# Start addresses of the x tiles in a fused gated attention and two-layer MLP kernel: four different residues of 512 bytes, or one

## The chip, the cores and the metric

One core of one Trainium2 chip runs the whole program. The metric is the device time of one execution in microseconds. Three runs of the kernel before gave 943.04, 944.69 and 944.89 us, median 944.69 us.

## The reference, cut to what matters

```python
f = 1.0 / (1.0 + np.exp(-f_logit))                      # q, k, v, f: (4, 8, 768, 48)
for t in range(S):
    state = f[:, :, t, :, None] * state + np.einsum('bhd,bhe->bhde', k[:, :, t], v[:, :, t])
    y[:, :, t] = np.einsum('bhd,bhde->bhe', q[:, :, t], state)
x = y.transpose(0, 2, 1, 3).reshape(3072, 384)
h = np.maximum(x @ w_in, 0.0)                           # (384, 2048)
x = h * h @ w_out                                       # (2048, 384)
h = x @ w2_in
g = np.where(h > 0.0, h, np.exp(np.minimum(h, 0.0)) - 1.0)
return g @ w2_out
```

The weights arrive as float64 and are decoded on the chip.

## The kernel before, in words

The 3072 tokens are cut into six blocks of 512, and each block passes through two layers. `BLOCKS` numbers them 0 to 5 (layer 0, whose x comes out of the attention) and 6 to 11 (layer 1, whose x is what layer 0 left in DRAM). Each block has 16 units, one for each 128 columns of the hidden width.

Precision is kept by splitting: x is held as a high and a low part (`xh`, `xl`, both of the type fp32r), so are the weights (`w`, `wf`) and the hidden values (`gh`, `gl`). A unit is 18 matmuls of TensorE, each with a stationary operand of 128 x 128 and a moving operand of 128 x 512:

- `up` (L343), nine matmuls into one PSUM bank `ph`: six whose moving operand is one of the three 512-column pieces of `xh`, each piece twice (with the high and the low weights), then three with the pieces of `xl`.
- `down` (L395), nine matmuls into three banks `y`: for each bank two with `gh` and one with `gl`.

Between the two, ScalarE, VectorE and GpSimd make `gh` and `gl` of `ph` (L356 to L382). The order of work is written out by hand. In slot u the loop at the end of `chunked` first runs what the table `plan` has for that slot (loads, the weights of layer 0 and 1, and a step of the chunked attention), then `up(u)`, then `down(u-2)`, then `between(u)` and `low(u)`. TensorE therefore sees up, down, up, down, and in layer 0 at some slots a piece of attention in front of `up`: either the scores (tp L166, sc L172) or the state and output (kv L201, y3p and yp L229 and L234).

The places in SBUF are set by the pools. A pool lays its tiles out one behind the other, and the pools follow each other in the order in which they are opened: `one`, `two`, `three`, `wpool`. The pool `two` gives every tag two buffers, so blocks with an even number use one `xh` and one `xl` buffer and odd blocks the other pair. `new_x` (L253 to L256) makes them: each tile has 16 columns of four bytes (64 bytes) more than it needs, and the views that the matmuls read begin behind these.

```python
tiles = [two.tile([128, NK * n + 16], F32R, tag=f"x{p}", name=f"x{p}{i}") for p in "hl"]
xr[i] = tuple(t[:, 16:].rearrange("r (k t) -> r k t", t=n) for t in tiles)
```

The views are filled by L263 and L269/L271 (layer 0) and by L280 and L281 (layer 1). The pieces within a view are 2048 bytes apart, so all three have the same residue.

Of the kernel before, what the change touches and what calls it, by code (L numbers as in the profile page):

```python
# [11 lines left out]
F32 = mybir.dt.float32  # L12
F32R = mybir.dt.float32r
# [12 lines left out]
NK = DM // 128  # L26
# [28 lines left out]
def chunked(ctx, tc, ff, qk, vk, vz, wraw, mask, ident, flag, out):  # L55
# [8 lines left out]

    one = ctx.enter_context(tc.tile_pool(name="one", bufs=1))
    two = ctx.enter_context(tc.tile_pool(name="two", bufs=2))
    three = ctx.enter_context(tc.tile_pool(name="three", bufs=3))
    wpool = ctx.enter_context(tc.tile_pool(name="wpool", bufs=NF))
    dram = ctx.enter_context(tc.tile_pool(name="dram", bufs=1, space=bass.MemoryType.DRAM))
# [11 lines left out]
    state = [one.tile([ROWS, NP, 48], F32, name=f"state{b}") for b in range(B)]  # L81
    diag = one.tile([ROWS, NP, ROWS], F32, name="diag")
    dlast = [one.tile([ROWS, NP], F32, name=f"dlast{b}") for b in range(B)]
    x2d = dram.tile([NK, 128, NT], F32, name="x2d")
    wst = dram.tile([NF, 128, 2, 2, DM], F32, name="wst")

    st = {}
    xr = {}
# [163 lines left out]

    def new_x(i):  # L253
        n = BLOCKS[i][2]
        tiles = [two.tile([128, NK * n + 16], F32R, tag=f"x{p}", name=f"x{p}{i}") for p in "hl"]
        xr[i] = tuple(t[:, 16:].rearrange("r (k t) -> r k t", t=n) for t in tiles)  # L256

    def a_hi(g):
        i, o = where[g]
        if o == 0:  # L260
            new_x(i)
        hi = xr[i][0][:, :, o:o + 128]
        A.activation(hi, st[g]["yp" if g < B else "x1"], AF.Copy)  # L263
# [9 lines left out]
    def load_x(i, k):  # L273
        layer, t0, n = BLOCKS[i]
        if k == 0:
            new_x(i)
        x = two.tile([128, n], F32, tag="x1", name=f"x2_{i}_{k}")
        nc.sync.dma_start(out=x, in_=x2d[k, :, t0:t0 + n])
        hi, lo = (a[:, k] for a in xr[i])
        V.tensor_copy(hi, x)  # L280
        V.tensor_tensor(out=lo, in0=x, in1=hi, op=ALU.subtract)  # L281
# [138 lines left out]
    for g in range(B, NG):  # L420
        i, o = where[g]
# [149 lines left out]
@with_exitstack  # L571
def gated_attention_moe(ctx: ExitStack, tc: tile.TileContext, ff, qk, vk, vz, nat, wraw, mask, ident, out):
    pool = ctx.enter_context(tc.tile_pool(name="flag", bufs=1))
    flag = pool.tile([1, 1], I32, name="flag")
    with ExitStack() as inner:
        chunked(inner, tc, ff, qk, vk, vz, wraw, mask, ident, flag, out)
    rv = tc.nc.values_load(flag[0:1, 0:1], min_val=0, max_val=1)
    with tc.If(rv == 1):
        with ExitStack() as inner:
            general(inner, tc, nat, wraw, ident, out)  # L580
# [56 lines left out]
```

## Time and profile before

| what | value |
|---|---|
| median of three runs | 944.69 us (943.04 to 944.89) |
| the profiled execution, device time | 943.66 us |
| its span, first to last instruction | 941.9 us |
| mean granted TensorE clock | 0.981 |
| PE busy, PEld busy | 913.2 us (97%), 740.8 us (79%) |
| VectorE, ScalarE, GpSimd busy | 564.4 us (60%), 455.8 us (48%), 327.1 us (35%) |
| chain that ended last, by engine | PE 87%, DVE 8%, issue 2% |

A matmul's duration in the profile overlaps that of the next one, so busy time says little about how close TensorE is to its rate. What is read below is the distance from the start of one matmul to the start of the next, which is the time that each one really takes of the program.

### The profile page before, as it was taken

The numbers are of one execution on the slowest core, as the hardware profiler recorded it, in microseconds if no ns is written. First come the engines' busy times: TensorE is split into PE (matmuls) and PEld (weight loads), VectorE is DVE, ScalarE is ACT, GpSimd is POOL, SyncE is SP. The second block draws the span as 40 slices with busy tenths as digits, with TensorE's granted clock in tenths as the row PEclk, the third lists the DMA queues.
The fourth block names the chain that finished last, engine by engine and source line by source line (L and its number), as shares of the span: only waits on it lengthen the run. The fifth ranks groups of instructions, "written<-read, shape, count | busy, mean of one in ns | idle before, by whom it ended". The sixth has DMA issues, their size and how long they took to land.

```text
span 941.9 us, 13099 instructions
## 1 busy us (share of the span) xinstructions
PE 913.2 (97%) x4841; PEld 740.8 (79%) x4841; DVE 564.4 (60%) x834; ACT 455.8 (48%) x791; POOL 327.1 (35%) x295
## 2 busy tenths in 40 slices
PE   6888989999999999999999999999999999999996
PEld 4766768888888888788888888888888888888885
DVE  8888886667667766775401166456555555555543
ACT  4457664554445445454444444444444444443543
POOL 5222323443444443444233232332332333233231
PEclk8799899999999999999999999999999999999998
DMA  8445423444433443442246530100100100100001
GB/s 277 141 141 192 131 67 123 135 137 141 141 108 109 143 142 126 154 146 78 94 158 213 174 135 1 57 12 1 56 12 1 56 13 0 57 12 1 34 0 37
DMA packets 30791, 88.44 MB, mean 94 GB/s; under 512 B 4992, under 2 KB 9728, under 8 KB 30720
## 3 DMA queue, kind: packets, MB, share of 16 engines
q1 hardware_dynamic: 28848, 77.32, 24.7%
q10 hardware_dynamic: 1872, 10.22, 3.2%
q8 instruction: 39, 0.64, 0.3%
q14 instruction: 32, 0.26, 0.1%
HBM read 64.52 MB, written 22.02 MB: 92 GB/s over the span
## 4 chain that ended last, share of the span: by engine, by line
PE 87%; DVE 8%; issue 2%; ACT 1%; DMA 1%; POOL 0%; ACTq 0%; DVEq 0%
PE y L395 40%; PE ph L343 40%; PE sc L172 2%; DVE dec L51 1%; DVE w L313 1%; PE yp L229 1%; PE yp L234 1%; DVE ds L136 1%; DVE dec L52 1%; PE kv L201 1%; DVE dec L48 1%; PE y3p L234 1%; DVE ss L181 1%; PE tp L166 1%; PE y3p L229 1%
## 5 line engine op out<-in xcount | busy, mean ns | idle before, releaser
L382 POOL TENSOR_TENSOR gl<-gg,gh 128x512 fp32r<-128x512 f32 x175 | 232.5, 1328 | 489.6 <-PE ph L343 193.5
L395 PE MATMUL y<-gh,w 128*128 128x512 f32 x576 | 179.9, 393 | 0.0
L395 PE MATMUL y<-gh,wf 128*128 128x512 f32 (+1 forms) x582 | 179.6, 390 | 0.0
L343 PE MATMUL ph<-xh,w 128*128 128x512 f32 x576 | 158.6, 410 | 11.2 <-ACT w L312 7.5
L368 DVE SCALAR_TENSOR_TENSOR t<-r,t 128x512 f32<-128x512 f32 (+1 forms) x97 | 71.5, 737 | 162.4 <-ACT r L367 161.3
L343 PE MATMUL ph<-xh,wf 128*128 128x512 f32 (+1 forms) x582 | 147.8, 389 | 0.0
L364 ACT ACTIVATE r<-ph 128x512 f32<-128x512 f32 (+1 forms) x97 | 57.6, 594 | 186.0 <-PE ph L343 176.7
L343 PEld LDWEIGHTS ph<-xh,w 128*128 128x128 f32 x576 | 107.1, 192 | 38.5 <-ACT w L312 9.2
L395 PEld LDWEIGHTS y<-gh,w 128*128 128x128 f32 x576 | 108.9, 189 | 24.9
L395 PEld LDWEIGHTS y<-gh,wf 128*128 128x128 f32 x582 | 108.9, 188 | 24.4 <-ACT gh L371 0.2
L343 PEld LDWEIGHTS ph<-xh,wf 128*128 128x128 f32 x582 | 108.6, 188 | 23.7
L395 PE MATMUL y<-gl,wf 128*128 128x512 f32 (+1 forms) x291 | 112.8, 388 | 0.0
L395 PE MATMUL y<-gl,w 128*128 128x512 f32 x288 | 112.5, 391 | 0.0
L356 ACT ACTIVATE r<-ph 128x512 f32<-128x512 f32 x96 | 56.9, 593 | 91.1 <-PE ph L343 73.5
L343 PE MATMUL ph<-xl,w 128*128 128x512 f32 x288 | 84.7, 403 | 0.2 <-DVE xl L269 0.2
L343 PE MATMUL ph<-xl,wf 128*128 128x512 f32 (+1 forms) x291 | 82.2, 391 | 0.0
L362 DVE TENSOR_TENSOR gh<-r 128x512 fp32r<-128x512 f32 x64 | 44.5, 696 | 48.6 <-ACT r L356 48.1
L369 DVE SCALAR_TENSOR_TENSOR gg<-ph,t 128x512 f32<-128x512 f32 (+1 forms) x97 | 66.6, 686 | 10.0
L343 PEld LDWEIGHTS ph<-xl,w 128*128 128x128 f32 x288 | 56.1, 195 | 13.2 <-DVE xl L269 0.6
L357 ACT ACTIVATE gg<-r 128x512 f32<-128x512 f32 x96 | 60.8, 633 | 8.0 <-ACT r L356 0.4
L395 PEld LDWEIGHTS y<-gl,wf 128*128 128x128 f32 x291 | 54.7, 188 | 12.1 <-DVE gl L376 0.2
L395 PEld LDWEIGHTS y<-gl,w 128*128 128x128 f32 x288 | 54.2, 188 | 12.4
(84 smaller groups left out, 1067.3 us busy)
## 6 DMA issues: line engine op xcount, KB each, us to landing
raw<-wraw SPq DMA_DIRECT2D x19, 768.0 KB, 4.5
wst<-w SPq DMA_DIRECT2D x16, 768.0 KB, 4.0
wf<-wst SPq DMA_DIRECT2D x16, 768.0 KB, 4.3
qk<-qk SPq DMA_DIRECT2D x24, 448.0 KB, 5.4
raw<-wraw ACTq DMA_DIRECT2D x13, 768.0 KB, 4.4
ff<-ff SPq DMA_DIRECT2D x22, 227.9 KB, 4.5
x2d<-yo SPq DMA_DIRECT2D x18, 256.0 KB, 2.3
x<-x2d SPq DMA_DIRECT2D x18, 256.0 KB, 3.1
```

The lines of the kernel that those rows point to most:

```text
L172: PE.matmul(sc[j][:, p], k[lo:hi, p], q[lo:hi, p], start=True, stop=True)
L229: PE.matmul(o[64 * j:64 * j + c.stop - c.start], v[:, c], ss[g % 2][:, j, p], start=p in (0, NK), stop=False, skip_group_check=True,)
L234: PE.matmul(o[:ROWS], diag[:, p], q[:, p], start=False, stop=p >= NK - 1, skip_group_check=True)
L343: PE.matmul(ph, w[:, a, 0, 128 * k:128 * k + 128], b[:, k, c], start=(m == 0), stop=(m == len(todo) - 1))
L356: A.activation(r[:, c], ph, AF.Relu)
L357: A.activation(gg[:, c], r[:, c], AF.Square)
L362: V.tensor_tensor(out=gh[:, c], in0=r[:, c], in1=r[:, c], op=ALU.mult)
L364: A.activation(r[:, c], ph, AF.Relu, scale=-1.0)
L368: V.scalar_tensor_tensor(out=t[:, c], in0=r[:, c], scalar=1.0, in1=t[:, c], op0=ALU.add, op1=ALU.mult)
L369: V.scalar_tensor_tensor(out=gg[:, c], in0=ph, scalar=0.0, in1=t[:, c], op0=ALU.max, op1=ALU.add)
L382: G.tensor_tensor(out=gl, in0=gg, in1=gh, op=ALU.subtract)
L395: PE.matmul(yp_[i][m][:, c], w[:, a, 1, 128 * m:128 * m + 128], b[:, c], start=(f == 0 and n_ == 0), stop=(f == NF - 1 and n_ == 2 and c.s ...
```

## The change

Two small tiles that nothing reads or writes are allocated, one of 64 bytes at the end of the part of the pool `one` that is laid out first, one of 192 bytes in a new pool `gap`, opened behind `two`. The x tiles lose their 64 bytes of margin.

```diff
     two = ctx.enter_context(tc.tile_pool(name="two", bufs=2))
+    gap = ctx.enter_context(tc.tile_pool(name="gap", bufs=1))
     three = ctx.enter_context(tc.tile_pool(name="three", bufs=3))
...
+    one.tile([128, 16], F32, name="shift")
+    gap.tile([128, 48], F32, name="shift2")
...
     def new_x(i):
         n = BLOCKS[i][2]
-        tiles = [two.tile([128, NK * n + 16], F32R, tag=f"x{p}", name=f"x{p}{i}") for p in "hl"]
-        xr[i] = tuple(t[:, 16:].rearrange("r (k t) -> r k t", t=n) for t in tiles)
+        tiles = [two.tile([128, NK * n], F32R, tag=f"x{p}", name=f"x{p}{i}") for p in "hl"]
+        xr[i] = tuple(t.rearrange("r (k t) -> r k t", t=n) for t in tiles)
```

No instruction is added, removed or moved: on every engine the sequence of operations, their shapes and the semaphores that they wait for are those of the kernel before. What differs is where operands start. The built programs place them so (start of the data, modulo 512 bytes):

| operand | before | after |
|---|---|---|
| `xh` of even blocks | 384 | 320 |
| `xl` of even blocks | 0 | 320 |
| `xh` of odd blocks | 320 | 320 |
| `xl` of odd blocks | 448 | 320 |
| `gh`, `gl` (all three buffers each), `yo` | 64 | 64 |
| weights `w`, `wf` (all sixteen buffers) | 64 | 64 |
| `qk` (both), the groups from 4 on | 256 | 320 |
| `vk`, `raw`, `dec`, `gg` (both buffers of each) | 0 | 320 |
| `ff` and `t` (first, second buffer) | 128, 192 | 192, 256 |
| `kt` | 352 | 416 |
| `r` | 96 | 160 |
| `x1` and `x2` staging (both) | 64 | 384 |
| `ss`, `diag`, `state`, `idt`, `msk`, `lim`, `ds` | unchanged | unchanged |

## Rows read from the trace of the kernel before

**Rows 1.** Busy time by stretch: us; PE, PEld, DVE, ACT, POOL busy (instructions); PEclk granted clock; DMA share, GB/s.
```profile
0.00:60.00 60.00, 46.77 (x354) 35.06 (x355) 50.41 (x73) 29.30 (x49) 22.24 (x30) 0.83 0.59 190
60.00:120.00 60.00, 54.82 (x341) 43.12 (x340) 52.70 (x81) 38.51 (x70) 20.72 (x19) 0.91 0.48 156
...
200.00:280.00 80.00, 80.00 (x490) 65.40 (x488) 54.06 (x80) 40.69 (x77) 34.30 (x35) 1.00 0.42 137
...
600.00:680.00 80.00, 80.00 (x351) 65.53 (x350) 44.99 (x69) 36.54 (x60) 24.66 (x19) 1.00 0.11 37
```

**Rows 2.** Chain of waits around 125 us: start us, us, engine, tile and line.
```profile
123.72 0.85 ACT w L312
124.60 0.97 DVE w L313
125.61 2.13 PE ph L343 x8
127.74 2.10 PE y L395 x9
```

**Rows 3.** TensorE in order of time, odd block 7: start us, us until the last end, group.
```profile
599.26 1.52 PE L343 MATMUL ph<-xh,wf 128*128 128x512 f32 x6
600.62 0.86 PE L343 MATMUL ph<-xl,wf 128*128 128x512 f32 x3
601.31 0.63 PE L395 MATMUL y<-gh,wf 128*128 128x512 f32 x2
...
602.01 0.62 PE L395 MATMUL y<-gh,wf 128*128 128x512 f32 x2
...
602.70 0.61 PE L395 MATMUL y<-gh,wf 128*128 128x512 f32 x2
...
603.38 0.39 PE L343 MATMUL ph<-xh,wf 128*128 128x512 f32 x1
```

**Rows 4.** The same view, first unit of even block 8.
```profile
665.18 1.55 PE L343 MATMUL ph<-xh,wf 128*128 128x512 f32 x6
666.57 0.85 PE L343 MATMUL ph<-xl,wf 128*128 128x512 f32 x3
667.26 0.63 PE L395 MATMUL y<-gh,wf 128*128 128x512 f32 x2
...
667.96 0.61 PE L395 MATMUL y<-gh,wf 128*128 128x512 f32 x2
...
668.64 0.61 PE L395 MATMUL y<-gh,wf 128*128 128x512 f32 x2
...
669.32 0.63 PE L343 MATMUL ph<-xh,wf 128*128 128x512 f32 x2
```

**Rows 5.** The same view, starts of blocks 6, 9, 10 and 11.
```profile
533.02 0.63 PE L343 MATMUL ph<-xh,wf 128*128 128x512 f32 x2
...
731.42 0.61 PE L343 MATMUL ph<-xh,wf 128*128 128x512 f32 x2
...
797.34 0.63 PE L343 MATMUL ph<-xh,wf 128*128 128x512 f32 x2
...
863.58 0.62 PE L343 MATMUL ph<-xh,wf 128*128 128x512 f32 x2
```

**Rows 6.** The same view, two groups of nine y matmuls behind each other, block 11.
```profile
927.52 0.62 PE L395 MATMUL y<-gh,wf 128*128 128x512 f32 x2
...
929.56 0.62 PE L395 MATMUL y<-gh,wf 128*128 128x512 f32 x2
...
931.60 0.40 PE L395 MATMUL y<-gh,wf 128*128 128x256 f32 x2
```

**Rows 7.** The same view, odd block 1, the unit behind an attention output.
```profile
180.92 0.85 PE L343 MATMUL ph<-xl,w 128*128 128x512 f32 x3
...
183.70 1.53 PE L343 MATMUL ph<-xh,w 128*128 128x512 f32 x6
185.06 0.86 PE L343 MATMUL ph<-xl,w 128*128 128x512 f32 x3
```

**Rows 8.** Chain of waits, attention pieces of one group of tokens each.
```profile
171.35 0.39 PE tp L166 x4
171.74 1.09 PE sc L172 x16
...
177.15 0.54 PE kv L201 x13
177.69 0.29 PE y3p L229 x4
177.98 0.66 PE yp L229 x12
178.64 0.40 PE y3p L234 x2
179.04 0.66 PE yp L234 x6
```

**Rows 9.** VectorE in order of time, t in two neighbouring units, so in both its buffers.
```profile
702.54 0.69 DVE L368 SCALAR_TENSOR_TENSOR t<-r,t 128x512 f32<-128x512 f32 x1 [2.12 <-ACT r L367]
...
706.68 0.69 DVE L368 SCALAR_TENSOR_TENSOR t<-r,t 128x512 f32<-128x512 f32 x1
```

**Rows 10.** Page, DMA issues: tiles, queue, count, KB each, us from issue to landing.
```profile
raw<-wraw SPq DMA_DIRECT2D x19, 768.0 KB, 4.5
...
wf<-wst SPq DMA_DIRECT2D x16, 768.0 KB, 4.3
```

## The prediction, made before the changed kernel was run

> **What bounds the kernel now.** I read the busy time by stretch first. From 200 us on PE is busy in all 80 of 80 us of a stretch at a granted clock of 1.00, the 2.4 GHz level, while DVE has 45 to 54 of 80 [rows 1]. In the first 120 us it is otherwise: PE is busy for 46.8 and 54.8 of 60 us, DVE for 50.4 and 52.7. The chain of waits agrees: it runs through the weight split on DVE up to 125.6 us and stays on PE from there [rows 2]. So a saving on PE counts from about 125 us to the end, and before that it counts nothing.
>
> A busy PE is not a PE at its best rate, so I went on to TensorE in order of time and took distances between starts. In odd block 7 the six matmuls on `xh` take 600.62 - 599.26 = 1.36 us, 226.7 ns each; the three on `xl` take 0.69; the nine on `gh` and `gl` take 603.38 - 601.31 = 2.07, in threes 0.70, 0.69 and 0.68 [rows 3]. The unit takes 4.12 us. In even block 8 the six take 1.39 us, 231.7 ns each, the three 0.69, the nine 2.06 (0.70, 0.68, 0.68), the unit 4.14 [rows 4]. The starts of the blocks say that this holds for all units: blocks 7 and 9 take 65.92 us, which is 16 x 4.12, and blocks 6, 8 and 10 take 66.24, which is 16 x 4.14 [rows 3 to 5].
>
> The same instructions with the same shapes, on the same weight buffers, thus differ by 5 ns with the block's parity, and the pair of x buffers is all that changes with it. `xh` starts at residue 384 in the slow case and at 320 in the fast one.
>
> Three things in these rows matter. First, 226.7 ns is the floor: the y matmuls settle there too (0.68 us for three). Second, where the stream stays at one residue it costs nothing more: two groups of nine y matmuls stand behind each other at the end, all at 64, and each takes 2.04 us, 226.7 ns a matmul from the first on [rows 6], though the bank changes every third matmul and `gh` changes between the groups. Third, a step from 64 to 320 is free (the six on `xh` of odd blocks, right behind the y group, are at the floor at once), while every step to or from 384, 448 or 0 is followed by slow matmuls, up to the first three to six of a y group. 64 and 320 are 256 apart; the other three residues are not a multiple of 256 away from 64.
>
> **The change part by part.** *The x tiles.* After the change all four are at 320. The six on `xh` in even blocks become those of the odd ones, which already stand there: 1.39 to 1.36 us, the surest part. The three on `xl` carry on at the residue of the six before them, so 3 x 226.7 = 0.68 us. The step from `xl` to the y group is then 320 to 64. No row has that one after full matmuls; its reverse is free, so I take it as free, and the y group as 2.04 us. A unit is then 18 x 226.7 ns = 4.08 us, against 4.14 (even, gain 0.06) and 4.12 (odd, gain 0.04).
>
> The sum over units:
> - Layer 1: blocks 6, 8 and 10 gain 3 x 16 x 0.06 = 2.88 us, blocks 7 and 9 gain 2 x 16 x 0.04 = 1.28. Block 11 has 14 units in the usual pattern (the last is cut in halves, and the y groups before it are at the floor already): 0.56. Together 4.72.
> - Block 5, odd, nearly without attention: 16 x 0.04 = 0.64.
> - Blocks 1 to 4: 64 units. About four in each block come right behind an attention output, and there the rate is lost for a while in any case: in odd block 1 the 12 matmuls from 180.92 to 183.70 take 231.7 ns each, and the next unit is at 1.36 us again for its six [rows 7]. I let these 16 units gain nothing. The other 48 gain 24 x 0.06 + 24 x 0.04 = 2.40.
> - Block 0: only what lies behind 125.6 us, some four units: 0.24.
>
> Sum 8.00 us.
>
> *The attention's matmuls.* `qk`, `vk` and `kt` move by 64 bytes (`vk` by 320) while `ss` and `diag` stay, so their relative places change and no row shows the new ones. The pieces of one group of tokens sum to 4.03 us [rows 8]; some 16 groups lie where PE sets the time, 64 us. The nearest rows are the two rates of the big matmuls, 226.7 and 231.7, or 2.2%: at most 1.4 us either way. I take nothing, since no row tells which way it would go.
>
> *The other engines.* `t` alternates between residues 128 and 192 and takes 0.69 us in both [rows 9]; I cost the moved operands of DVE, ACT and POOL at nothing. PE's work covers them from 125 us on. In the first 125 us they have no such cover, and a change of 1% of DVE's 103 us there would be 1 us either way.
>
> *DMA.* `raw` and its like move from 0 to 320. Loads of the same 768 KB land in 4.5 us at residue 0 (`raw`) and in 4.3 us at 64 (`wf`) [rows 10], a 0.2 us difference that includes queueing; loads are issued two units ahead, so nothing.
>
> *Nothing else.* The two gap tiles have no instruction. No queue has a new entry and no wait is added.
>
> The profiled execution took 943.66 us, so the sum gives 935.7. The median of the runs stands 1.03 us above that execution, and 8.0 off it would be 936.7; I give **936.0**.
>
> **A rule that speaks against it.** The rows show `xh` at 384 at 231.7 ns and at 320 at 226.7 [rows 3, 4]. The Trainium skill (SBUF — State Buffer, "Who interferes with whom") says that PE has two SBUF read ports of its own, one for the moving operand and one for the weight load, and never waits on anyone. By that, a start address would be worth nothing and the sum would be 0. The trace does not agree with it in full, by those 5 ns.
>
> **The rivals.**
> 1. *The y groups keep their slow start.* The step from x to g also changes the PSUM bank and brings the waits for `gh` (DVE) and `gl` (POOL). If these cost the first y matmuls their time, only `up` gains: even 2.08 to about 2.05 us, odd nothing (there the slow `xl` steps, 0.01 us, are within rounding). That is 76 even units (48 in layer 1, 24 in blocks 1 to 4, 4 in block 0) x 0.03 = 2.3 us, a time of 941.4. Against it: two y groups behind each other have the same waits and bank changes and start at the floor [rows 6]. For it: no row shows full matmuls stepping from 320 to 64.
> 2. *Addresses are worth nothing*, and the parity of the block acts in some other way, for example by which physical part of SBUF the buffers lie in. Time 943.7. Against it: odd `xh` stays at the very address that it has now, and even `xh` moves by 64 bytes only. The rule above is this rival's.
> 3. *The slow pattern locks in, and the kernel is slower.* Behind an attention output an odd block ran a whole unit at 231.7 ns, through `xl` at 448 and all nine y matmuls, and came back only at the next `xh` [rows 7]. Perhaps a change of residue is what resets it. With one residue throughout, a stream once out of step would then stay so: 18 x 231.7 = 4.17 us a unit, 0.03 more than now in 76 even units and 0.05 more in 86 odd ones, 2.3 + 4.3 = 6.6 us, time 950.3. It decides once over 55% of the units are in that state, since 8.0 x 0.45 is about 6.6 x 0.55. Against it: y groups at one residue settle at the floor by their fourth to seventh matmul in layer 1, without any change of residue [rows 3, 4].
> 4. *The tiles do not get the places that the change names.* The built program has all four at 320; no chance.
>
> **How the numbers follow.** Forecast 0.70, rival 1 0.15, rival 2 0.07, rival 3 0.08. The range: below, the forecast with the attention's 1.4 us in its favour and the units behind attention gaining as well, 935.7 - 1.4 - 1.0, or 933; above, rival 1 with half a microsecond of scatter, 942. Rivals 2 and 3 stay outside. About 0.2% (1.9 us) is what a measurement of this kernel can tell from no change. Rival 1 at 2.3 us lies near that border and is split: faster 0.80, same 0.13, slower 0.07.
>
> **What would show it.** Right: in layer 1 every block takes 65.3 us (16 x 4.08), odd and even alike; six on `xh` 1.36, three on `xl` 0.68, y groups 2.04. If `up` falls to 2.05 and y stays at 2.06, it is rival 1; odd at 65.9 and even at 66.2, rival 2; all at 66.7, rival 3. What lies before 125 us should stay as it is, and the attention's pieces at 4.03 us a group. The prediction is wrong in its core if the y group's first three matmuls still take 0.70 us.

## The result, and the profile after

The changed kernel takes 935.28 us (median of six runs, 933.91 to 936.75) against 944.57 us of the kernel before (six runs, 942.65 to 945.27): ratio 0.9907, 95% interval 0.9892 to 0.9922, or 9.3 us faster. The forecast was 936.0 us with a range from 933 to 942.

The profiled execution took 934.45 us, its span is 932.7 us. The first fence is TensorE in order of time (start us, us until the last end, group) for the first unit of odd block 7 and the starts of the blocks; it answers to [rows 3 to 5].

```profile
141.43 0.62 PE L347 MATMUL ph<-xh,w 128*128 128x512 f32 x2
...
463.63 0.62 PE L347 MATMUL ph<-xh,w 128*128 128x512 f32 x2
...
529.04 0.61 PE L347 MATMUL ph<-xh,wf 128*128 128x512 f32 x2
...
594.32 1.52 PE L347 MATMUL ph<-xh,wf 128*128 128x512 f32 x6
595.68 0.84 PE L347 MATMUL ph<-xl,wf 128*128 128x512 f32 x3
596.36 0.61 PE L399 MATMUL y<-gh,wf 128*128 128x512 f32 x2
...
598.40 0.39 PE L347 MATMUL ph<-xh,wf 128*128 128x512 f32 x1
...
659.60 0.61 PE L347 MATMUL ph<-xh,wf 128*128 128x512 f32 x2
...
855.44 0.62 PE L347 MATMUL ph<-xh,wf 128*128 128x512 f32 x2
```

The six on `xh` take 1.36 us, the three on `xl` 0.68, the y group 598.40 - 596.36 = 2.04: all 18 matmuls of the unit are at the floor of 226.7 ns, the shortest distance that any of these matmuls settles at. Blocks 6 and 7 take 65.28 us each, and blocks 8 to 10 together 855.44 - 659.60 = 195.84, three times that.

To place the rest, the next fence has the starts of blocks 1 and 5 and the last matmul of the kernel before in the same view, and the one behind it the last matmul after.

```profile
142.18 0.62 PE L343 MATMUL ph<-xh,w 128*128 128x512 f32 x2
...
466.97 0.62 PE L343 MATMUL ph<-xh,w 128*128 128x512 f32 x2
...
934.10 0.28 PE L395 MATMUL y<-gl,wf 128*128 128x256 f32 x1
```

```profile
925.38 0.28 PE L399 MATMUL y<-gl,wf 128*128 128x256 f32 x1
```

| stretch | before, us | after, us | gain | predicted |
|---|---|---|---|---|
| up to the start of block 1 | 142.18 | 141.43 | 0.75 | 0.24 |
| blocks 1 to 4 | 324.79 | 322.20 | 2.59 | 2.40 |
| block 5 | 66.05 | 65.41 | 0.64 | 0.64 |
| blocks 6 to 10 | 330.56 | 326.40 | 4.16 | 4.16 |
| block 11 to its last matmul | 70.52 | 69.94 | 0.58 | 0.56 |
| behind the last matmul | 7.8 | 7.3 | 0.5 | 0 |

### The profile page after: what moved, and what is told of

It is laid out like the page before. It is cut to its first block, busy times and chain, and to the rows that moved or that the text cites. A ratio compares the mean times of both kernels' runs of the same rounds, so it can differ in the third digit from the quotient of the medians.

```text
span 932.7 us, 13099 instructions
## 1 busy us (share of the span) xinstructions
PE 899.2 (96%) x4841; PEld 735.5 (79%) x4841; DVE 565.3 (61%) x834; ACT 456.1 (49%) x791; POOL 326.8 (35%) x295
## 4 chain that ended last, share of the span: by engine, by line
PE 89%; DVE 6%; issue 1%; DMA 1%; ACT 1%; POOL 1%; ACTq 0%; SPq 0%; DVEq 0%
PE ph L347 41%; PE y L399 41%; PE sc L176 2%; PE yp L238 1%; PE yp L233 1%; DVE w L317 1%; DVE ds L140 1%; DVE dec L51 1%; DVE dec L52 1%; PE kv L205 1%; PE y3p L238 1%; PE y3p L233 1%; PE tp L170 1%; ACT w L316 1%; DMA raw<-wraw 0%
## 5 line engine op out<-in xcount | busy, mean ns | idle before, releaser
L399 PEld LDWEIGHTS y<-gh,wf 128*128 128x128 f32 x582 | 108.9, 188 | 22.4 <-ACT gh L375 0.2
L347 PE MATMUL ph<-xl,w 128*128 128x512 f32 x288 | 82.8, 396 | 0.8 <-DVE xl L273 0.8
```

Of the source, the lines that this page charges most:

```text
L347: PE.matmul(ph, w[:, a, 0, 128 * k:128 * k + 128], b[:, k, c], start=(m == 0), stop=(m == len(todo) - 1))
L399: PE.matmul(yp_[i][m][:, c], w[:, a, 1, 128 * m:128 * m + 128], b[:, c], start=(f == 0 and n_ == 0), stop=(f == NF - 1 and n_ == 2 and c.s ...
```

## The experiments

What was open: whether the x tiles alone do it; whether x has to agree with `gh` and `gl`, its neighbours in the stream, or with the weights; how exact the agreement has to be and with what period; and which half of the change carries what. Every kernel differs from the changed one only in where tiles start, unless said otherwise. "Off" means the distance of a moving operand's start from that of the weights, modulo 256 bytes; "in place" means 0 off; matmuls are "in step" when they follow each other at 226.7 ns. In the views called chain of waits, the numbers are the start in us and the us that the piece takes of the chain.

**Run xonly: the x tiles alone.** Small pads inside the pool `two` put x at 320 and leave every other tile at the residue that it had before.

```diff
+            if g == 0:
+                two.tile([128, 8], F32, tag="pad", name="pad0")
...
+            if g == 2:
+                two.tile([128, 24], F32, tag="pad2", name="pad2")
...
-        tiles = [two.tile([128, NK * n + 16], F32R, tag=f"x{p}", name=f"x{p}{i}") for p in "hl"]
+        tiles = [two.tile([128, NK * n], F32R, tag=f"x{p}", name=f"x{p}{i}") for p in "hl"]
```

> All four x tiles at 320, and every other tile at the residue it had in the kernel before (raw, vk, dec, gg at 0, qk at 256). If the x tiles alone do it: unit 4.08 us in every block of layer 1, block 65.28 us, time 935.3 us within 1.5. If the other tiles that the change moved carry part of it: between 936.5 and 944.6, with units of layer 1 above 4.08.

Measured 936.58 us, ratio to the kernel before 0.9910 (0.9884 to 0.9937). Chain of waits in block 8:

```profile
670.98 2.04 PE ph L347 x9
673.02 2.04 PE y L399 x9
```

The unit is 4.08 us. The x tiles alone carry the gain; the places of `raw`, `vk`, `dec`, `gg` and the others had no part that these times resolve. In the traces one small difference is left: in block 1 an `up` behind scores takes 2.24 us here and 2.26 in the changed kernel.

**Runs x384 and x448: one residue for x, but another one.** The sizes of the two gap tiles are exchanged for others of the same sum (32 and 32 columns, 48 and 16), so x lies 64 and 128 off.

```diff
-    one.tile([128, 16], F32, name="shift")
-    gap.tile([128, 48], F32, name="shift2")
+    one.tile([128, 32], F32, name="shift")
+    gap.tile([128, 32], F32, name="shift2")
```

> All four x tiles at one residue, 384, which is 64 off the residue of gh, gl and the weights modulo 256. If one common residue for x were enough: 4.08 us a unit, 935 us. If x must agree with gh, gl or the weights modulo 256: the six xh matmuls near 1.39 us as in even blocks of the kernel before, a slow start of each y group, unit 4.12 to 4.17 us, time 941 to 951.

> All four x tiles at 448, 128 off the residue of gh, gl and the weights modulo 256. If the period is 128 bytes: 4.08 us a unit, 935 us. If it is 256: units of 4.12 to 4.17 us, 941 to 951.

Measured 945.26 us (1.0027, 1.0012 to 1.0041) and 947.51 us (1.0043, 1.0030 to 1.0057). Chain of waits in block 8, first x384, then x448:

```profile
672.30 2.08 PE y L399 x9
674.38 2.06 PE ph L347 x9
```

```profile
673.70 2.07 PE y L399 x9
675.76 2.09 PE ph L347 x9
```

One common residue for x is worth nothing by itself, and 128 bytes is no period. In x384 the y group, whose own operands have not moved, takes 2.08 us, more than the 2.06 and 2.07 that it took before [rows 3, 4]: what `up` leaves behind slows it.

**Run w128: only the weights moved.** A gap of 64 bytes in front of the pool `wpool`; x stays at 320, `gh` and `gl` at 64, so the moving operands agree with each other as in the change and all are 192 off the weights.

```diff
+    gap2 = ctx.enter_context(tc.tile_pool(name="gap2", bufs=1))
     wpool = ctx.enter_context(tc.tile_pool(name="wpool", bufs=NF))
...
+    gap2.tile([128, 16], F32, name="shift3")
```

> As the change, but all sixteen weight buffers at residue 128 in place of 64; x stays at 320, gh and gl at 64. If only the moving operands have to agree with each other modulo 256: nothing changes, 4.08 us a unit, 935.3 us. If each moving operand has to agree with the weights loaded meanwhile: all 18 matmuls of a unit lose the floor, 18 x 231.7 ns = 4.17 us, 0.09 us in some 175 units, 951 us. If that relation also sets the floor itself, the unit may come out below 4.08 or above 4.17.

Measured 955.00 us, ratio 1.0119 (1.0094 to 1.0144): slower than both kernels. TensorE in order of time, first unit of block 7, and from the page the group of the y group's weight loads (busy us, mean ns):

```profile
604.36 1.56 PE L349 MATMUL ph<-xh,wf 128*128 128x512 f32 x6
...
606.46 0.63 PE L401 MATMUL y<-gh,wf 128*128 128x512 f32 x2
...
608.56 0.63 PE L349 MATMUL ph<-xh,wf 128*128 128x512 f32 x2
```

```profile
L401 PEld LDWEIGHTS y<-gh,wf 128*128 128x128 f32 x582 | 109.0, 188 | 25.9
```

The unit takes 608.56 - 604.36 = 4.20 us, 233.3 ns a matmul, worse than the 4.12 and 4.14 of the kernel before in layer 1. So it is not enough that the moving operands agree among themselves: the place of the weights counts for all 18. A weight load still takes 188 ns, as in the kernel before, whose page has 108.9 us and a mean of 188 ns for this group; what grows is the distance between matmuls, not the load.

**Run ss64: the attention's operands at the common residue too**, and everything from x on 256 bytes further, so that x is at 64 and the weights, `gh` and `gl` at 320.

```diff
+    one.tile([128, 24], F32, name="shift0")
     ss = [one.tile([128, 2, NP, 128], F32, name=f"ss{i}") for i in range(2)]
...
-    one.tile([128, 16], F32, name="shift")
-    gap.tile([128, 48], F32, name="shift2")
+    one.tile([128, 56], F32, name="shift")
+    gap.tile([128, 48], F32, name="shift2")
```

> As the change, but ss and diag (moving and stationary operands of the attention's output matmuls) also at the common residue modulo 256: ss, diag, qk, vk, x at 64, gh, gl and the weights at 320 modulo 512. Layer 1 as in the change, 65.28 us a block, since every pair of x, g and weights keeps its distance modulo 256. If the unit behind an attention output (2170 ns for its nine up matmuls in place of 2040) is slow because of where ss and diag lie, blocks 1 to 4 fall by up to four times 0.13 us each, 2 us in all; if it is the interruption itself that puts the stream out of step, they stay at 82.5, 82.5, 81.6 and 75.6 us, and the time at 935 us.

Measured 936.61 us, ratio 0.9919 (0.9897 to 0.9941). Chain of waits in block 1, a unit behind scores and the next behind an output, first the changed kernel, then ss64:

```profile
213.09 2.26 PE ph L347 x9
215.35 2.04 PE y L399 x9
...
219.93 2.09 PE ph L347 x9
```

```profile
215.34 2.26 PE ph L348 x9
217.60 2.04 PE y L400 x9
...
222.19 2.09 PE ph L348 x9
```

The pieces are the same to 0.01 us. So 256 bytes more on every operand change nothing, and moving `ss` and `diag` does nothing for the `up` behind an attention output, which stays at 2.09. The interruption, not the place of its operands, is the likelier cause, though `kt` was not at the common residue here and nothing else about the interruption was varied.

One rival is left open by this run and all others. Wherever a unit runs at the floor, x, `gh`, `gl` and the weights all stand at 64 modulo 256 bytes; no run put moving operands and weights together at another residue. So it is not shown whether the two operands have to agree with each other, or each has a good place of its own that happens to be the same. What follows speaks of agreement; the second reading fits the same rows.

**Run sweep: how exact.** The x of each block starts at another distance; `yo` has two buffers for three, to make room.

```diff
+OFF = 0, 8, 240, 112, 80, 208, 16, 32, 48, 96, 160, 224
...
+        o = OFF[i] // 4
-        tiles = [two.tile([128, NK * n], F32R, tag=f"x{p}", name=f"x{p}{i}") for p in "hl"]
-        xr[i] = tuple(t.rearrange("r (k t) -> r k t", t=n) for t in tiles)
+        tiles = [two.tile([128, NK * n + 64], F32R, tag=f"x{p}", name=f"x{p}{i}") for p in "hl"]
+        xr[i] = tuple(t[:, o:o + NK * n].rearrange("r (k t) -> r k t", t=n) for t in tiles)
...
-                y = three.tile([128, n], F32, tag="yo", name=f"yo{i}_{m}")
+                y = yop.tile([128, n], F32, tag="yo", name=f"yo{i}_{m}")
```

> As the change, but the x of block i starts 0, 8, 240, 112, 80, 208, 16, 32, 48, 96, 160, 224 bytes (i = 0 to 11) behind an address that equals 64 modulo 256, so 0 to 240 off the weights; the yo staging tiles have two buffers for three, which makes the room. If what counts is the moving operand's place against the weights modulo 256 with a best point at equality: the nine up matmuls take 2.04 us only where the offset is 0 and more at every other one (2.06 at 64 and 2.10 at 128 and 192 were measured, so 2.05 to 2.11 here). If equality is not the best point, some offset gives less than 2.04 us. If only 64-byte steps count, offsets 8, 16, 32 and 48 give 2.04.

One execution, 954.65 us; the two `yo` buffers are part of that, so only the groups inside blocks are read. Chain of waits, one `up` group each of blocks 1, 2, 4, 7, 9 and 10, whose x is 8, 240, 80, 32, 96 and 160 off, with the y group behind it for 240, 32 and 160:

```profile
168.40 2.09 PE ph L350 x9
...
252.29 2.10 PE ph L350 x9
254.39 2.04 PE y L402 x9
...
418.99 2.07 PE ph L350 x9
...
613.03 2.10 PE ph L350 x9
615.13 2.08 PE y L402 x9
...
767.79 2.11 PE ph L350 x9
...
827.19 2.10 PE ph L350 x9
829.30 2.04 PE y L402 x9
```

In the same view `up` takes 2.08, 2.09, 2.10, 2.11 and 2.10 us at 16, 112, 48, 208 and 224 off (blocks 6, 3, 8, 5 and 11). No distance but 0 gives 2.04 us; 8 bytes off already cost 0.05, and the usual price is 0.06. Zero is a sharp point and not the middle of a basin. With 64 and 128 from the two runs above, the mildest distances for `up` are 64 (2.06) and 80 (2.07).

What an `up` out of place leaves behind depends on its distance as well. Behind x 160, 224 or 240 off the y group takes 2.04 us in this view, close to the floor, and behind 208 it takes 2.05; behind 8, 16, 32, 48, 80, 96 and 112 it takes 2.06 to 2.09. A unit then costs about 4.15 us at 160, 224 and 240, as it does at 64. The runs do not show why.

**Runs hi_only and lo_only: half of the change each.** They use the kernel of sweep with distances by parity for `xh` and `xl`: (0, 0) and (192, 128) in hi_only, (64, 0) and (0, 0) in lo_only, for even and odd blocks.

> Half of the change: xh of all blocks at the residue of the weights modulo 256, xl left at the distances it had before (192 off in even blocks, 128 off in odd ones); yo has two buffers for three. If the y group's slow start is carried over from xl being out of place, it stays: odd blocks of layer 1 exactly as before, 65.92 us, even ones down from 66.24 to about 65.9, and the time near 941 us, a third of the change's gain. If only the places of xh matter: 65.3 us a block and 935 us.

> The other half: xl of all blocks at the residue of the weights modulo 256, xh left as before (64 off in even blocks, 0 off in odd ones); yo has two buffers for three. If what counts is the place of each operand against the weights and the state of the stream is carried from group to group: odd blocks of layer 1 as in the change, 65.28 us, with y groups of 2.04 us; even blocks between 65.3 and 66.2, xh still at 1.39 us, and the y groups faster than 2.06 if the three xl matmuls are enough to fall into step. Time 937 to 940 us.

Measured 948.66 us (1.0051, 1.0034 to 1.0068) and 947.39 us (1.0035, 1.0021 to 1.0050), both slower than the kernel before. These times do not answer the question: the two `yo` buffers delay block ends, as the next pair shows.

**Runs hi_half and lo_half: the halves with all three `yo` buffers.** The room comes from smaller gaps (16 columns for `shift2`) and margins of 48 columns in `xl`, or 16 in `xh` and 32 in `xl` (`MORE` is then `(16, 32), (0, 32)`).

```diff
+MORE = (0, 48), (0, 32)
...
+        more, odd = MORE
+        tiles = [two.tile([128, NK * n + m], F32R, tag=f"x{p}", name=f"x{p}{i}") for p, m in zip("hl", more)]
+        os = [m * (i % 2) for m in odd]
+        xr[i] = tuple(t[:, o:o + NK * n].rearrange("r (k t) -> r k t", t=n) for t, o in zip(tiles, os))
```

> The xh half of the change without the delay at block ends: xh at the residue of the weights modulo 256 in all blocks, xl 192 off in even and 128 off in odd blocks as before, yo with its three buffers. If xl out of place brings back the slow start of the y groups in every unit: 65.92 us in every block of layer 1 (4.12 a unit: up 2.06, y 2.06), so 0.02 us gained in some 76 even units, 1.5 us in all, about 943 us where the kernel before has 944.5.

> The xl half without that delay: xl at the residue of the weights modulo 256 in all blocks, xh 64 off in even and 0 off in odd blocks as before, yo with its three buffers. Odd blocks of layer 1 at 65.28 us as in the change; even ones at 66.56, slower than the 66.24 before, since xl and y start out of step behind xh and the y groups then need 2.07 us. Gain 0.04 us in some 86 odd units, loss 0.02 in some 76 even ones, together about 2 us: 942.5 us. The two halves by themselves would then come to 3.5 us, the whole to 9.

Measured 943.18 us (0.9993, 0.9979 to 1.0008) and 941.94 us (0.9978, 0.9965 to 0.9991). Chain of waits, first hi_half in even block 8, then lo_half in odd block 7 and even block 8:

```profile
670.09 2.06 PE ph L350 x9
672.14 2.06 PE y L402 x9
```

```profile
601.75 2.04 PE ph L350 x9
603.79 2.04 PE y L402 x9
...
671.27 2.09 PE ph L350 x9
673.36 2.07 PE y L402 x9
```

With `xl` out of place every y group keeps its slow start; with `xh` out of place the three `xl` matmuls, though in place, do not fall into step, and the y group behind them is slower than before (2.07 against 2.06, [rows 4]). In the medians the halves come to 0.5 (not clear of nothing) and 1.8 us, 2.3 together; the whole is 9.3. The traces say the same without the scatter of the start (TensorE in order of time, first matmul of block 1 and last of the program, first hi_half, then lo_half):

```profile
143.15 1.53 PE L350 MATMUL ph<-xh,w 128*128 128x512 f32 x6
...
934.08 0.28 PE L402 MATMUL y<-gl,wf 128*128 128x256 f32 x1
```

```profile
141.44 1.52 PE L350 MATMUL ph<-xh,w 128*128 128x512 f32 x6
...
931.12 0.28 PE L402 MATMUL y<-gl,wf 128*128 128x256 f32 x1
```

Between the two lie 790.93 and 789.68 us, in the kernel before 791.92 and in the changed one 783.95: 1.0 and 2.2 for the halves, 8.0 for the whole. hi_half gains less than the 1.5 us expected of it. The gain needs `xh` and `xl` in place together.

The pair also prices the confound. hi_only less hi_half is 5.5 us and lo_only less lo_half 5.4 us; since the two pairs were measured at different times, the safer figure is against the kernel before at each time (944.31 and 943.72 us), which makes it 4.9 us in both. The two of each pair differ in the number of `yo` buffers and, besides, in where `raw` and its neighbours lie, which xonly showed to be worth nothing that its time resolves.

**Run wdown128: two halves of the weights.** The part of each weight tile that y uses starts 64 bytes further, the part that `up` uses stays; `yo` has one buffer.

```diff
+    def apart(t):
+        return t[:, :1568].rearrange("r (i q) -> r i q", i=2)[:, :, :768].rearrange("r i (a m) -> r i a m", a=2)
...
+            t = apart(wpool.tile([128, 1600], F32R, tag="w", name=f"w{layer}_{f}"))
```

> As the change, but the half of each weight tile that the y matmuls use lies 64 bytes further (128 modulo 256), the half that the up matmuls use stays at 64; yo has one buffer for three, which delays block ends. If each group must agree with its own weights: y groups at 2.10 us in the pattern of 231 and 236 ns that all weights at 128 gave, and up groups that have to fall into step anew in every unit, 2.04 to 2.09 us; unit 4.14 to 4.19. If agreement in one of the two groups were enough to hold the stream in step: 4.08.

One execution, 985.6 us; TensorE waits 17.9 us of it for `yo`, so only the groups inside a block are read. TensorE in order of time, inside block 8:

```profile
700.43 1.53 PE L358 MATMUL ph<-xh,wf 128*128 128x512 f32 x6
701.80 0.84 PE L358 MATMUL ph<-xl,wf 128*128 128x512 f32 x3
702.48 0.63 PE L410 MATMUL y<-gh,wf 128*128 128x512 f32 x2
...
703.19 0.63 PE L410 MATMUL y<-gh,wf 128*128 128x512 f32 x2
```

`up` takes 702.48 - 700.43 = 2.05 us, 0.01 above the floor, and the first three y matmuls 0.71. Agreement is a matter of each group and its weights. Whether a matmul must agree with the weights that it uses or with those that are loaded while it streams can be asked only where a group ends, since elsewhere both lie at one residue. The trace leans to the weights in use: the load of the first y weights starts at 702.26, while the last of the three `xl` matmuls streams, and these three still take 702.48 - 701.80 = 0.68 us, the floor.

## Why the prediction was right, point by point

**The rate of a unit.** The prediction's 18 x 226.7 ns = 4.08 us is what every undisturbed unit takes. The step that had no row, from `xl` at 320 to the y group, is free as assumed. Blocks 6 to 10, block 5 and block 11 came out at 4.16, 0.64 and 0.58 us against 4.16, 0.64 and 0.56.

**The reason, as the prediction put it, was half of it.** It spoke of steps between residues of the stream, with 64 and 320 as 256 apart. The period holds, but the place of the weights counts as well, as w128 shows: the stream there has the same residues as in the change and lost 20 us against it. That the weights lie at 64 like `gh` and `gl` hid the difference; on the rows before, both readings give 4.08 us, so the forecast did not depend on which was right.

**One row was read too far.** Two y groups at the floor behind half-width `xl` matmuls [rows 6] were taken to show that a stream at one residue costs nothing more. The `xl` in front of them stood at 448, and by the prediction's next sentence a step from there makes the first y matmuls slow, so the row spoke against that sentence too. After the change, with everything in place, the first of these groups takes 0.70 us for its first three (TensorE in order of time, block 11):

```profile
918.79 0.63 PE L399 MATMUL y<-gh,wf 128*128 128x512 f32 x2
...
919.49 0.63 PE L399 MATMUL y<-gh,wf 128*128 128x512 f32 x2
```

Behind a change of width the state of the stream is not known, in place or not.

**The sum.** 8.0 us were forecast; the profiled executions differ by 943.66 - 934.45 = 9.2. Of the missing 1.2, 0.5 lies before block 1, 0.5 behind the last matmul and 0.2 in blocks 1 to 4. The start of block 1 is no measure of the change: in the profile of xonly, whose x has the same places, it is 144.70 us (TensorE in order of time), 3.3 later, and it is 143.15 in hi_half and 141.44 in lo_half.

```profile
144.70 0.62 PE L347 MATMUL ph<-xh,w 128*128 128x512 f32 x2
```

Behind the last matmul nothing of x is left, and what follows it there takes 7.0 us in hi_half and 7.4 in lo_half (spans 941.1 and 938.5). So about 1 us of the 9.2 is scatter that fell on the good side. Where x acts, from the start of block 1 to the last matmul, the gain is 791.92 - 783.95 = 7.97 us, against the 7.76 that were forecast for that stretch. The medians fit that: the change stands at 9.3, and the other two kernels with every x at 0 off, xonly and ss64, lie 7.2 and 7.3 us below the kernel before as measured with them.

**Units behind an attention output.** They were counted at no gain. They gain some 0.03 us each (mean of blocks 1 to 4), since the stream is back in step sooner. The unit of [rows 7] ran at 231.7 ns a matmul from 180.92 to 183.70; now (TensorE in order of time, block 1) the 12 matmuls from 179.92 to 182.66 take 228.3 ns each, the y group 2.04 us:

```profile
179.92 0.86 PE L347 MATMUL ph<-xl,w 128*128 128x512 f32 x3
180.62 0.62 PE L399 MATMUL y<-gh,w 128*128 128x512 f32 x2
...
182.66 1.52 PE L347 MATMUL ph<-xh,w 128*128 128x512 f32 x6
```

**Units behind scores.** The prediction did not set these apart, about four a block as well, and counted them at the full 0.04 and 0.06 us. Their `up` is interrupted too and hardly gains. In block 1 of the kernel before (chain of waits) such a unit takes 2.25 + 2.06 us:

```profile
172.83 2.25 PE ph L343 x9
175.09 2.06 PE y L395 x9
```

In the changed kernel it takes 2.26 + 2.04, shown under ss64: 0.01 us gained where 0.04 was counted (0.03 where 0.06 was, in the even blocks). By the means of the traces the two misses are 0.4 to 0.5 us each, with opposite signs; that blocks 1 to 4 came to 2.59 us against 2.40 is luck to that extent.

**The attention's own matmuls**, bounded at 1.4 us either way, did not change: sc 1.09 and yp 0.66 us a piece as in [rows 8].

**Rival 1** (y groups keep their slow start) is excluded by 2.04 us for the y groups of blocks 6 to 10, whose 16 units take 65.28 us a block. **Rival 2** (addresses are worth nothing) falls with 9.3 us, and with xonly, where x alone stands at another residue. So does, for this kernel, what the prediction drew from the rule of the Trainium skill (SBUF — State Buffer, "Who interferes with whom"), that a start address would be worth nothing: the weight load keeps its 188 ns and the matmuls' distance moves between 226.7 and 233.3 ns with the two operands' places. Whether moving operand and weight load meet at a port the runs do not show. **Rival 3** (the slow pattern locks in) did not come about here, but w128 looks like it: with the stream nowhere in place it never falls into step, and a unit takes 4.20 us, where the rival had 4.17.

## What to carry to other kernels

Where TensorE runs 128 x 512 fp32r matmuls back to back, start every moving operand at the residue of the weights modulo 256 bytes, all of them: here that was worth 0.9%, either half of it alone about 0.2% or less, and the weights 64 bytes off cost 1.2%. The residue at which all stood here was 64; another common one was not tried. Look for it by start-to-start distances per buffer, since busy time and the weight loads' durations don't show it. Before paying for such a placement with a buffer, price the buffer: one `yo` buffer fewer cost some 5 us, about half of what the placement gives.

## What the runs showed of the hardware that was not expected

The time from one matmul to the next depends on where the moving operand and the weights start, modulo 256 bytes, and a shift of 8 bytes, the finest tried, already counts: nine matmuls take 2.04 us with both at the same residue (64 in every run) and 2.06 to 2.11 at the fourteen other distances given above. It has a memory: from out of step it takes up to some ten matmuls in place to come to 226.7 ns (three in [rows 4], next to none behind an `up` 160, 224 or 240 off in sweep), and it stays there until something out of place or another kind of matmul intervenes. Whether the two places have to agree or each has a good one of its own, which operand is read at which moment, and why 226.7 ns is the floor, no run here shows.
